# First pair's softmax ahead of the first weight conversion, and one more raw buffer, in a fused attention and two-stage MoE kernel

## Chip, cores and metric

The kernel runs on one core of a Trainium2 chip. The metric is the time of one execution on the device in microseconds. All times of the trace are microseconds from the start of the profiled span unless ns stands beside them. TensorE, VectorE, ScalarE and GpSimd are PE, DVE, ACT and POOL in the rows; SP issues the DMAs; PEld is the load of stationary operands.

## The reference, cut to what matters

```
scores = (q @ k.T) / 8; masked by blocks of 64 positions (block_i >= block_j)
attn   = softmax(scores) @ v                     # 4 batches, 8 heads, 576 x 64
x      = attn as [2304 tokens, 512]
x      = (sigmoid(x @ w_gate) * (x @ w_val)) @ w_out         # 512 -> 1536 -> 512
p      = domain_probs / (sum of domain_probs + 1e-9)
out    = sum over 4 experts e: p[:, e] * (relu(x @ w1[e]) @ w2[e])   # 512 -> 1024 -> 512
```

The inputs q, k and the MoE weights are float64 or float32 arrays; `w_gate`, `w_val` and `w_out` arrive as 64-bit words.

## The kernel before, in words

Three stages are interleaved on one core. **Attention** goes in 16 pairs of heads (4 batches of 4 pairs); a pair has query tiles t = 0 to 4 of 128 tokens (the last has 64). For each tile TensorE makes scores (line 350 for the first two batches), VectorE fills the masked corner (line 380) and takes the negative maximum (line 381, for t=4 line 411), ScalarE exponentiates with a running sum (lines 383, 416), TensorE transposes the probabilities (lines 459, 479), ScalarE copies them out of PSUM (line 446) and TensorE multiplies by v (line 532 through the helper at 119). Lines 491 to 510 prepare the inverse sums, line 541 writes the pair's output for batch 0. Steps of a pair are staggered: the transposes of a tile come three steps, the product with v four steps behind its scores, so steps of the next pair stand in between.

**The first MoE** works in four passes of 576 tokens (one batch each). Each pass has 12 blocks f of 128 hidden columns for gate and value. A block is one Winograd step of seven products; its weights come as four tiles a, b, c, d of high and low halves, made by `conv_items` (line 641): two raw blocks of 512 KB are loaded (line 647), decoded from 64-bit words by `from_f64` (lines 614 on ScalarE, 615 and 616 on VectorE), summed on GpSimd (line 662), split into high and low halves (`split_sb`, lines 124 to 133) and stored to DRAM (line 670) for later passes. Blocks 0 to 4 are converted during the attention of batch 0, the others during the first pass, which takes the blocks in the order `FIRST = (4, 0, 5, 1, 6, 2, 7, 3, 8, ...)`. Output weights are loaded raw and converted in `wo_get` (line 685). All raw tiles have the tag `raw` with three buffers in pool `conv`.

The operands of a pass are made by `x1_prep` (line 745) through `winograd_left`: four loads for each of two halves, sums on GpSimd (line 727), splits on ScalarE and VectorE (tiles `xc`). The first pass takes them from SBUF, the second pass loads them from DRAM into tiles `xr1` with four buffers (lines 752 to 757), the third and fourth have their own way (`x1_early`). **The second MoE** follows in three passes of 768 tokens.

What sets the order: the list `queue` holds the attention's steps with a place each (batch number plus the share of its cost so far); `attn_to(x)` runs them up to place x. At lines 1302 to 1305 the attention runs to place 0.12, and then the rest of batch 0 (to 1.05) is merged by cost with the 60 conversion steps of the first five blocks, 12 to a block. From there the attention is paced by the first MoE's progress (line 1359). Each engine executes its own instructions strictly in order; that order is drawn up when the kernel is built, by a planner that goes by the order in the text and a simulated timeline, so an instruction can be placed ahead of one that stands earlier in the text. A step wrapped in `pinned` (line 102) stays behind the instruction before it on VectorE, ScalarE and GpSimd. A tile's first writer waits until a buffer of its tag is free.

Of the kernel before, what the change touches and what calls it, by code (L numbers as in the profile page):

```python
# [8 lines left out]
F32 = mybir.dt.float32  # L9
F32R = mybir.dt.float32r  # L10
I32 = mybir.dt.int32
# [7 lines left out]
NC0 = 5  # L19
FIRST = (4, 0, 5, 1, 6, 2, 7, 3, 8, 9, 10, 11)  # L20
A00 = 0.12
A1 = [1.05, 2.3, 4, 4, 4]
PACE1 = 0.9
GB = 4
# [1 line left out]
LATE = (0, 1, 2)  # L26
LN = 1
ORD = "stvn"
RAW_BUFS = 3
PT2_BUFS = 1  # L30
LT, LP = 3, 4
PTB = 3
# [30 lines left out]
def attention_moe_moe_kernel(  # L63
# [18 lines left out]
    P = 128  # L82
    BLK = 64
    NKT = DM // P
    NF = DFF // P
# [50 lines left out]
    moe1 = tc.alloc_tile_pool(name="moe1", bufs=1)  # L136
    conv = tc.alloc_tile_pool(name="conv", bufs=1)
# [485 lines left out]
    TH1 = TP1 // 2  # L623
# [17 lines left out]
    def conv_items(f):  # L641

        d = {}

        def raw(gv):
            t = d["raw", gv] = conv.tile([P, NKT, P, 2], I32, tag="raw", name="raw", bufs=3)
            nc.sync.dma_start(
                out=t.rearrange("p c f t -> p c (f t)"),
                in_=(w_gate, w_val)[gv].bitcast(I32)[:, 2 * f * P:2 * (f + 1) * P].rearrange("(c p) f -> p c f", p=P))

        def f64(gv):
            d[gv] = from_f64(d["raw", gv].rearrange("p c f t -> p (c f) t"))

        def b(k, a):
            return d[a][:, k * QF:(k + 1) * QF]

        def sums(n):
            if n == 0:
                d["t"] = conv.tile([P, 4, QF], F32, tag="wt", name="wt")
            t = d["t"]  # L660
            x, y = [(b(0, 1), b(0, 0)), (b(1, 1), t[:, 0]), (b(1, 1), b(0, 1)), (b(1, 0), t[:, 1])][n]
            nc.gpsimd.tensor_tensor(out=t[:, n], in0=x, in1=y, op=ALU.subtract)

        def part(k):
            t = w1_tile(k)
            src = dict(a=lambda: d[0], b=lambda: d["t"][:, 0:2].rearrange("p n f -> p (n f)"),
                       c=lambda: d["t"][:, 2:4].rearrange("p n f -> p (n f)"), d=lambda: b(1, 1))[k]()
            split_sb(t[:, 0].rearrange("p n f -> p (n f)"), t[:, 1].rearrange("p n f -> p (n f)"), src,
                     "p" if k in "bc" else "a", "v" if k == "a" else "p")
            nc.sync.dma_start(out=w1_at(f, k), in_=t.bitcast(F32))  # L670
            if f >= NC0 - 1:
                wg[f, k] = t

        r = [lambda: raw(0), lambda: raw(1), lambda: f64(0), lambda: f64(1), lambda: sums(0), lambda: part("a"),
             lambda: sums(1), lambda: part("b"), lambda: sums(2), lambda: sums(3), lambda: part("c"), lambda: part("d")]
        return [(1.0, x) for x in r]
# [8 lines left out]
    def wo_get(p, f):  # L685
        t = wo[f] = moe1.tile([P, 2, DM], F32R, tag="wo", name="wo", bufs=4)
        if p:
            nc.sync.dma_start(out=t.bitcast(F32), in_=wo_d[f])
            return
        raw = conv.tile([P, NKT, P, 2], I32, tag="raw", name="raw", bufs=3).rearrange("p c f t -> p (c f) t")  # L690
        nc.sync.dma_start(out=raw.rearrange("p d t -> p (d t)"), in_=w_out.bitcast(I32)[f * P:(f + 1) * P, :])
        split_sb(t[:, 0], t[:, 1], from_f64(raw), "a", "p")
        nc.sync.dma_start(out=wo_d[f], in_=t.bitcast(F32))
# [18 lines left out]
    def winograd_left(pool, dst, load, n):  # L712
# [29 lines left out]
                    r.append((0.0, lambda kk=kk, m=m, key=key: part(kk, m, key)))  # L742
        return r

    def x1_prep(p):
        def load(kk, t, h):
            kt = h * KH + kk
            while (p, "b", kt) not in x_d:
                attn_next()
            if p == 0:  # L750
                return x0[kt][:, t]
            r = moe1.tile([P, TH1], F32, tag="xr1", name="xr1", bufs=4)
            if t == 0:
                nc.sync.dma_start(out=r[:, :QA], in_=x_d[p, "a", kt])
                nc.sync.dma_start(out=r[:, QA:], in_=x_d[p, "b", kt][:, :TH1 - QA])
            else:
                nc.sync.dma_start(out=r, in_=x_d[p, "b", kt][:, TH1 - QA:])
            return r

        return winograd_left(moe1, xc1, load, TH1)  # L760
# [145 lines left out]
    def run(lst):  # L906
        for _, fn in lst:
            fn()

    if True:  # L910
# [353 lines left out]
        for x in range(3):  # L1264
            t = (attn if x < 2 else pt2).tile([P, S], F32R, tag="kl" if x < 2 else "kl2", name=f"klz{x}", bufs=2 if x < 2 else 1)
# [3 lines left out]
        for x in range(2):  # L1269
            t = attn.tile([P, 5, 2, D], F32, tag="vh", name=f"vh{x}", bufs=2)  # L1270
            nc.vector.memset(t[64:128, 4], 0.0)
            vts.append(t)
        for x in range(PTB):
            t = (attn if x < 2 else pt2).tile([P, 1280], F32, name=f"pTb{x}")
# [23 lines left out]
        def attn_to(target):  # L1298
            while pos[0] < len(queue) and place[pos[0]] < target:
                attn_next()  # L1300

        attn_to(A00)
        a0 = [(queue[i][2], attn_next) for i in range(pos[0], len(queue)) if place[i] < A1[0]]
        cs = [conv_items(f) for f in range(NF)]
        _merge(a0, sum(cs[:NC0], []), 1.0)
        x_items = x1_prep(0)
        prev = []
        for p in range(NP1):
            at, total = 0.0, NF * 7 * 6 * C1 + NF * 2 * NKT * 3 * C1
            for f0 in range(0, NF, 2):  # L1310
                if (p, f0) == (NP1 - 1, 2):
                    x1b.release()
                    p2r = tc.alloc_tile_pool(name="p2r", bufs=1, side="right", reuse_waits="tile")
                    wp = [w_prep(0), w_prep(1)]
                    pre = x_prep(0) + [(0.0, lambda: (w_load(0), w_load(1), p_prep()))] + wp[0] + wp[1][:-2] + [(0.0, lambda: w2_load(0))]
                items = []
                for f in (f0, f0 + 1):
                    fa = order[p][f]
                    it = l1_1(p, fa)
                    side = []  # L1320
                    if (p, f) != (NP1 - 1, NF - 1):
                        nf = order[p][f + 1] if f + 1 < NF else order[p + 1][0]
                        if p == 0 and f + 1 < NF and nf >= NC0:
                            side += [x for _, x in cs[nf][HEAD:]]
                        else:
                            side.append(lambda nf=nf: w1_load(nf))
                    side.append(lambda fa=fa: wo_get(p, fa))
                    if p == 0 and f + 2 < NF and order[0][f + 2] >= NC0:
                        side += [x for _, x in cs[order[0][f + 2]][:HEAD]]
                    if p == NP1 - 1 and f >= 2:  # L1330
                        side += [pinned(x) for _, x in pre[len(pre) * (f - 2) // (NF - 3):len(pre) * (f - 1) // (NF - 3)]]
                    m = len(it)
                    steps = list(it)
                    for n in reversed(range(len(side))):
                        it.insert(1 + n * m // len(side), (0.0, side[n]))
                    if p in (1, 2) and f >= NF - 2:
                        if f == NF - 2:
                            if p == 1:
                                attn_to(99)
                                x1b = tc.alloc_tile_pool(name="x1b", bufs=1, side="right", reuse_waits="tile")  # L1340
                            first, part = x1_early(p + 1, x1b)
                            for n, fn in enumerate(first):
                                it.insert(1 + n, (0.0, fn))
                        else:
                            for n, x in enumerate(steps):
                                it.insert(it.index(x) + 1, (0.0, lambda n=n: part(ORD1[n])))
                    items += it
                if f0 == 0 and p < 2:
                    items = x_items + items
                if f0 == NF - 2 and p == 0:  # L1350
                    x_items = x1_prep(p + 1)
                    n = len(items)
                    for m in range(4):
                        items.insert(n * 2 // 3 + m, x_items[m])
                    x_items = x_items[4:]
                both = []
                _merge([(x[0], lambda x=x: both.append(x)) for x in items], [(x[0], lambda x=x: both.append(x)) for x in prev])
                for c, fn in both:
                    attn_to(A1[p] + (A1[p + 1] - A1[p]) * min(1.0, at / total / PACE1))
                    fn()  # L1360
                    at += c
                if (p, f0) == (0, NF - 2):
                    conv.release()
                prev = l2_1(p, f0)
        run(prev)
# [6 lines left out]
        for p in range(NPASS):  # L1372
            for q0 in range(0, NQ, 2):
# [22 lines left out]
                n = len(items)  # L1396
# [48 lines left out]
```

## Time and profile before

| what | before |
|---|---|
| median of 3 runs | 1411.94 us (1411.53 to 1413.97) |
| the profiled execution's own time | 1413.05 us |
| its span, first to last instruction | 1411.3 us |
| mean granted TensorE clock | 0.993 of full speed |
| busy: TensorE / its loads / VectorE / ScalarE / GpSimd | 1372.7 / 1267.3 / 986.3 / 777.6 / 481.5 us |
| DMA | 369.57 MB, 262 GB/s in the mean |

The profile is of one execution. Busy time of TensorE is modelled for pipelined matmuls and says little of how full it is where it waits often; the waits (in brackets in a timeline row: idle time before the instruction, and what ended it) say more.

### The profile page before, as it was taken

How to read it: one execution, taken by the hardware profiler on the slowest of the kernel's cores; microseconds unless marked ns; L12 is line 12 of the kernel's file. 1: busy time of each engine (PE TensorE's matmuls, PEld its weight loads, DVE VectorE, ACT ScalarE, POOL GpSimd, SP SyncE). 2: the span in 40 equal slices, each digit the busy share in tenths (PEclk: the TensorE clock that was granted, in tenths of full speed). 3: DMA queues.
4: the chain of work that ended last, by engine and by line, in shares of the span. 5: the costliest groups of instructions: out<-in, count | busy, mean ns of one | idle time of the engine just before them, and what ended most of it. 6: DMA issues, size and time to landing. Idle time of an engine off the chain costs nothing.

```text
span 1411.3 us, 26204 instructions
## 1 busy us (share of the span) xinstructions
PE 1372.7 (97%) x9212; PEld 1267.3 (90%) x9212; DVE 986.3 (70%) x2103; ACT 777.6 (55%) x1926; POOL 481.5 (34%) x502
## 2 busy tenths in 40 slices
PE   6899999999999999999999999999999999999998
PEld 3467787889988999999999999989999999999998
DVE  6877689976776445466777666757766787766766
ACT  5888788888876333343445444544444454443442
POOL 4753346301122200022576556533222342322322
PEclk8999999999999999999999999999999999999999
DMA  7999677886657877998799888886666777676754
GB/s 224 299 285 294 214 237 249 267 238 201 194 165 226 298 262 268 319 341 299 273 340 350 298 301 305 288 301 232 232 251 241 258 259 283 245 270 229 275 206 157
DMA packets 210803, 369.57 MB, mean 262 GB/s; under 512 B 74736, under 2 KB 137200, under 8 KB 204528
## 3 DMA queue, kind: packets, MB, share of 16 engines
q1 hardware_dynamic: 209584, 367.62, 77.2%
q8 instruction: 74, 1.21, 0.3%
q14 instruction: 57, 0.47, 0.1%
q10 hardware_dynamic: 1088, 0.26, 0.1%
HBM read 267.82 MB, written 100.01 MB: 261 GB/s over the span
## 4 chain that ended last, share of the span: by engine, by line
PE 86%; DVE 4%; DMA 4%; ACT 3%; issue 1%; SPq 1%; POOL 1%; DVEq 0%; ACTq 0%; POOLq 0%
PE c L119 38%; PE o L119 26%; PE lo L119 7%; PE s L119 4%; PE obank L119 3%; PE t L119 3%; PE tbank L459 2%; DMA raw<-in_moe_w_val_dram 1%; PE s L350 1%; PE tbank L230 1%; PE tbank L479 1%; DVE raw L616 1%; DMA w1g<-w1d 1%; DVE nm L381 0%; ACT pt L383 0%
## 5 line engine op out<-in xcount | busy, mean ns | idle before, releaser
L119 PE MATMUL c<-xc,w1g 128*128 128x384 f32 x1920 | 384.6, 338 | 1.5 <-DMA w1g<-w1d 1.2
L119 PEld LDWEIGHTS c<-xc,w1g 128*128 128x128 f32 x1920 | 330.5, 188 | 7.7 <-DVE hb L1073 1.4
L119 PE MATMUL o<-w2s,hb 128*128 128x256 f32 x1728 | 243.5, 282 | 1.1 <-DVE acc L1222 1.1
L119 PEld LDWEIGHTS o<-w2s,hb 128*128 128x128 f32 x1728 | 231.8, 189 | 2.0 <-DVE acc L1222 1.7
L1222 DVE SCALAR_TENSOR_TENSOR acc<-o,pr_t,acc 128x256 f32<-128x256 f32 x264 | 123.4, 479 | 57.9 <-PE o L119 55.8
L1082 POOL TENSOR_TENSOR hs<-hf 128x384 f32<-128x384 f32 x64 | 64.0, 1022 | 287.5 <-ACT hf L1090 256.4
L119 PE MATMUL lo<-g,wo 128*128 128x288 f32 x888 | 150.8, 301 | 5.0 <-DVE x L895 3.0
L119 PE MATMUL o<-w,hb 128*128 128x512 f32 x576 | 142.8, 391 | 0.0
L119 PEld LDWEIGHTS lo<-g,wo 128*128 128x128 f32 x888 | 126.4, 188 | 11.0 <-DVE x L895 5.1
L1090 ACT ACTIVATE hf<-c 128x384 f32<-128x384 f32 x128 | 65.7, 513 | 115.1 <-DVE c L1127 57.8
L119 PEld LDWEIGHTS o<-w,hb 128*128 128x128 f32 x576 | 107.2, 188 | 18.5 <-DVE acc L1166 0.2
L1127 DVE TENSOR_TENSOR c<-c,snap 128x384 f32<-128x384 f32 x144 | 77.8, 552 | 56.0 <-PE c L119 38.4
L1120 ACT ACTIVATE snap<-c 128x384 f32<-128x384 f32 x144 | 65.7, 484 | 87.1 <-PE c L119 86.8
L1071 ACT ACTIVATE hb<-hs 128x384 fp32r<-128x384 f32 x128 | 63.3, 518 | 64.4 <-POOL hs L1082 64.2
L1073 DVE TENSOR_TENSOR hb<-hs,hb 128x384 fp32r<-128x384 f32 x128 | 87.2, 696 | 5.5 <-ACT hb L1071 5.2
L895 DVE TENSOR_TENSOR x<-lo,x 128x288 f32<-128x288 f32 x124 | 55.7, 453 | 45.7 <-PE lo L119 44.9
L119 PE MATMUL c<-xc,wa 128*128 128x288 f32 x504 | 83.9, 300 | 1.8 <-ACT xc L131 1.6
L383 ACT ACTIVATE pt<-s,nm 128x128 f32<-128x128 f32 (+3 forms) x128 | 67.5, 529 | 17.9 <-DVE nm L381 10.7
L119 PEld LDWEIGHTS c<-xc,wa 128*128 128x128 f32 x504 | 71.8, 189 | 4.2 <-ACT xc L131 2.2
L119 PE MATMUL c<-xc,wc 128*128 128x288 f32 x432 | 70.8, 298 | 0.4 <-ACT snap L819 0.4
L819 ACT ACTIVATE snap<-c 128x288 f32<-128x288 f32 x108 | 44.4, 411 | 41.4 <-PE c L119 41.0
L459 PE MATMUL tbank<-ident,pt 128*128 128x128 f32 x320 | 53.6, 282 | 12.5 <-ACT pTa L446 7.7
(180 smaller groups left out, 2707.1 us busy)
## 6 DMA issues: line engine op xcount, KB each, us to landing
w1g<-w1d SPq DMA_DIRECT2D x96, 512.0 KB, 5.3
w2s<-w2d SPq DMA_DIRECT2D x48, 1024.0 KB, 6.2
w1d<-w1g SPq DMA_DIRECT2D x48, 512.0 KB, 4.9
wa<-w1d SPq DMA_DIRECT2D x40, 512.0 KB, 5.0
wb<-w1d SPq DMA_DIRECT2D x40, 512.0 KB, 5.1
wc<-w1d SPq DMA_DIRECT2D x40, 512.0 KB, 4.3
wo<-wod SPq DMA_DIRECT2D x36, 512.0 KB, 5.8
wr<-in_moe_w_dram SPq DMA_DIRECT2D x32, 512.0 KB, 5.4
```

The source lines that it names most:

```text
L119: ins = nc.tensor.matmul(out=out, lhsT=lhsT, rhs=rhs, start=start, stop=stop, skip_group_check=skip)
L383: ins = nc.scalar.activation(out=pt[:, x * nk:(x + 1) * nk], in_=sp[:, x - x0], func=AF.Exp, bias=nm[:, j0 + x:j0 + x + 1], scale=1.0, acc ...
L459: nc.tensor.transpose(out=tbank[:, x * P:(x + 1) * P], in_=pt[:, x * P:(x + 1) * P], identity=ident)
L819: nc.scalar.activation(out=t, in_=d["c1"][:, :TH1], func=AF.Copy)
L895: nc.vector.tensor_tensor(out=x2[t, dm], in0=ps, in1=x2[t, dm], op=ALU.add)
L1071: nc.scalar.activation(out=t[:, 0], in_=src, func=AF.Copy if low is None else AF.Relu)
L1073: nc.vector.tensor_tensor(out=t[:, 1], in0=src, in1=t[:, 0].bitcast(F32), op=ALU.subtract)
L1082: nc.gpsimd.tensor_tensor(out=o, in0=x, in1=y, op=op)
L1090: nc.scalar.activation(out=hf[q, blk], in_=c, func=AF.Relu)
L1120: nc.scalar.activation(out=t, in_=d["c1"][:, :TH], func=AF.Copy)
L1127: nc.vector.tensor_tensor(out=c, in0=d[tag][:, :TH], in1=d[n], op=ALU.add)
L1222: nc.vector.scalar_tensor_tensor(out=o, in0=ps, scalar=pr, in1=o, op0=ALU.mult, op1=ALU.add)
```

## The change

The attention runs to place 0.12, then the first block's two raw loads are issued, then the attention runs on to place 0.25 (`A01`), which takes in the last scores of pair 0, most of its transposes and the scores of pair 1's tiles 0 to 2. The remaining ten conversion steps of block 0 and all of blocks 1 to 4 are merged with the rest of batch 0's attention; block 0's two decoding steps are pinned behind what precedes them. The tag `raw` has four buffers. The second pass's operand loads lose their own tag: two of them share one raw tile (each takes 288 of its 1024 32-bit columns), and pool `conv` is released after the second pass's first pair of blocks instead of at the end of the first pass.

```diff
--- before.py
+++ after.py
@@ -19,6 +19,7 @@
 NC0 = 5
 FIRST = (4, 0, 5, 1, 6, 2, 7, 3, 8, 9, 10, 11)
 A00 = 0.12
+A01 = 0.25
 A1 = [1.05, 2.3, 4, 4, 4]
 PACE1 = 0.9
 GB = 4
@@ -26,7 +27,7 @@
 LATE = (0, 1, 2)
 LN = 1
 ORD = "stvn"
-RAW_BUFS = 3
+RAW_BUFS = 4
 PT2_BUFS = 1
 LT, LP = 3, 4
 PTB = 3
@@ -643,7 +644,7 @@
         d = {}
 
         def raw(gv):
-            t = d["raw", gv] = conv.tile([P, NKT, P, 2], I32, tag="raw", name="raw", bufs=3)
+            t = d["raw", gv] = conv.tile([P, NKT, P, 2], I32, tag="raw", name="raw", bufs=RAW_BUFS)
             nc.sync.dma_start(
                 out=t.rearrange("p c f t -> p c (f t)"),
                 in_=(w_gate, w_val)[gv].bitcast(I32)[:, 2 * f * P:2 * (f + 1) * P].rearrange("(c p) f -> p c f", p=P))
@@ -687,7 +688,7 @@
         if p:
             nc.sync.dma_start(out=t.bitcast(F32), in_=wo_d[f])
             return
-        raw = conv.tile([P, NKT, P, 2], I32, tag="raw", name="raw", bufs=3).rearrange("p c f t -> p (c f) t")
+        raw = conv.tile([P, NKT, P, 2], I32, tag="raw", name="raw", bufs=RAW_BUFS).rearrange("p c f t -> p (c f) t")
         nc.sync.dma_start(out=raw.rearrange("p d t -> p (d t)"), in_=w_out.bitcast(I32)[f * P:(f + 1) * P, :])
         split_sb(t[:, 0], t[:, 1], from_f64(raw), "a", "p")
         nc.sync.dma_start(out=wo_d[f], in_=t.bitcast(F32))
@@ -742,6 +743,8 @@
                     r.append((0.0, lambda kk=kk, m=m, key=key: part(kk, m, key)))
         return r
 
+    xw = {}
+
     def x1_prep(p):
         def load(kk, t, h):
             kt = h * KH + kk
@@ -749,7 +752,11 @@
                 attn_next()
             if p == 0:
                 return x0[kt][:, t]
-            r = moe1.tile([P, TH1], F32, tag="xr1", name="xr1", bufs=4)
+            if t == h:
+                t2 = conv.tile([P, NKT, P, 2], I32, tag="raw", name="xr1", bufs=RAW_BUFS)
+                xw[0] = t2.bitcast(F32).rearrange("p c f t -> p (c f t)")
+            o = 0 if t == h else TH1
+            r = xw[0][:, o:o + TH1]
             if t == 0:
                 nc.sync.dma_start(out=r[:, :QA], in_=x_d[p, "a", kt])
                 nc.sync.dma_start(out=r[:, QA:], in_=x_d[p, "b", kt][:, :TH1 - QA])
@@ -1300,8 +1307,11 @@
                 attn_next()
 
         attn_to(A00)
+        cs = [conv_items(f) for f in range(NF)]
+        run(cs[0][:2])
+        attn_to(A01)
+        cs[0] = [(c, pinned(fn) if n < 2 else fn) for n, (c, fn) in enumerate(cs[0][2:])]
         a0 = [(queue[i][2], attn_next) for i in range(pos[0], len(queue)) if place[i] < A1[0]]
-        cs = [conv_items(f) for f in range(NF)]
         _merge(a0, sum(cs[:NC0], []), 1.0)
         x_items = x1_prep(0)
         prev = []
@@ -1359,7 +1369,7 @@
                     attn_to(A1[p] + (A1[p + 1] - A1[p]) * min(1.0, at / total / PACE1))
                     fn()
                     at += c
-                if (p, f0) == (0, NF - 2):
+                if (p, f0) == (1, 0):
                     conv.release()
                 prev = l2_1(p, f0)
         run(prev)
```

## Rows read from the trace of the kernel before

**Rows 1.** TensorE's busy tenths in 40 slices of the span, on the page.

```profile
PE   6899999999999999999999999999999999999998
```

**Rows 2.** Busy us by stretch: PE, PEld, DVE, ACT, POOL (instructions), clock, DMA share, GB/s.

```profile
17.00:27.00 10.00, 3.11 (x16) 1.94 (x15) 9.30 (x19) 7.04 (x17) 7.03 (x8) 0.62 0.92 257
27.00:47.00 20.00, 16.65 (x97) 9.41 (x95) 18.40 (x45) 15.76 (x49) 15.64 (x18) 0.85 0.91 301
47.00:67.00 20.00, 17.00 (x113) 9.66 (x114) 16.77 (x51) 16.65 (x57) 13.42 (x15) 1.00 0.94 286
67.00:87.00 20.00, 17.81 (x116) 10.81 (x116) 16.59 (x42) 16.88 (x54) 14.76 (x17) 1.00 1.03 344
107.00:200.00 93.00, 91.69 (x645) 73.52 (x645) 70.11 (x180) 75.92 (x214) 34.52 (x35) 1.00 0.79 253
200.00:280.00 80.00, 76.07 (x549) 66.87 (x548) 74.27 (x178) 69.04 (x189) 36.66 (x35) 1.00 0.78 256
```

**Rows 3.** Timeline, opening: start, length, engine, line, what [idle before, releaser].

```profile
12.44 3.89 PE L350 MATMUL s<-tkn,tqn 64*64 64x288 f32 x12
...
16.93 0.43 DVE L615 TENSOR_SCALAR raw<-raw 128x512 int32<-128x512 int32 x1 [3.66 <-DMA raw<-in_moe_w_gate_dram]
...
17.27 0.45 DVE L411 TENSOR_REDUCE nm<-s 128x1 f32<-128x288 f32 x1
...
23.30 0.38 SPq L647 DMA_DIRECT2D raw<-in_moe_w_val_dram  x1
...
24.03 0.90 PE L459 MATMUL tbank<-ident,pt 128*128 128x128 f32 x3 [6.89 <-ACT pTa L446]
...
27.58 0.67 ACT L614 ACTIVATE raw<-raw 128x512 f32<-128x512 f32 x1 [1.10 <-DMA raw<-in_moe_w_val_dram]
...
34.75 0.56 DVE L381 TENSOR_REDUCE nm<-s 128x1 f32<-128x384 f32 x1
```

**Rows 4.** Timeline: block 4's last weights on POOL, and first pass products on TensorE.

```profile
73.34 1.28 POOL L133 TENSOR_TENSOR wc<-wt,wc 128x512 fp32r<-128x512 f32 x1
...
90.85 0.64 PE L119 MATMUL c<-xc,wa 128*128 128x288 f32 x3
...
97.26 1.02 PE L119 MATMUL c<-xc,wc 128*128 128x288 f32 x6 [0.41 <-ACT snap L819]
```

**Rows 5.** Groups of ScalarE, 13 to 46 us: busy, mean ns; idle before.

```profile
L383 ACT ACTIVATE pt<-s,nm 128x384 f32<-128x384 f32 (+3 forms) x12 | 6.7, 561 | 1.0 <-DVE nm L381 1.0
...
L446 ACT ACTIVATE pTb<-tbank 128x384 f32<-128x384 f32 (+3 forms) x9 | 3.5, 425 | 0.0
...
L383 ACT ACTIVATION_READ_ACCUMULATOR pt<-s,nm 128x1 f32 x12 | 2.5, 205 | 0.0
...
L416 ACT ACTIVATE pt<-s,nm 128x288 f32<-128x288 f32 x4 | 2.0, 496 | 2.4 <-DVE nm L413 2.4
```

**Rows 6.** Groups of VectorE, 0 to 87 us, same columns.

```profile
L381 DVE TENSOR_REDUCE nm<-s 128x1 f32<-128x128 f32 (+3 forms) x36 | 16.5, 470 | 0.5
...
L616 DVE SCALAR_TENSOR_TENSOR raw<-raw 128x512 int32<-128x512 int32 x13 | 10.8, 840 | 0.3
...
L615 DVE TENSOR_SCALAR raw<-raw 128x512 int32<-128x512 int32 x13 | 7.2, 551 | 3.9 <-DMA raw<-in_moe_w_gate_dram 3.8
...
L133 DVE TENSOR_TENSOR wa<-raw,wa 128x512 fp32r<-128x512 f32 x5 | 4.8, 960 | 0.0
```

**Rows 7.** The raw tiles, whole span: ns min/median/max, first and last start.

```profile
L615 DVE TENSOR_SCALAR raw<-raw x36: 412/424/1491, 16.9 to 252.7; 128x512 int32<-128x512 int32 x36
...
L616 DVE SCALAR_TENSOR_TENSOR raw<-raw x36: 660/692/1659, 17.6 to 253.3; 128x512 int32<-128x512 int32 x36
...
L647 SPq DMA_DIRECT2D raw<-in_moe_w_val_dram x12: 368/384/972, 12.4 to 232.0; - x12
...
DMA to landing us min/median/max: 3.6/5.3/8.2
```

**Rows 8.** Tile xr, 90 to 300 us: first split of the second pass's operands.

```profile
L131 ACT ACTIVATE xc<-xr x6: 443/454/496, 263.0 to 276.9; 128x288 fp32r<-128x288 f32 x6
```

## The prediction

> **What bounds the kernel now.** I read the page first, for where TensorE is not full. Its row of 40 slices stands at 9 from the third slice to the last but one and is lower only in the first two [rows 1]: what can be won lies in the opening 70 us and in the first pass's start behind them. Next, the windows [rows 2]. From 27 to 87 us TensorE is nominally 83 to 89% busy, but VectorE is the fuller one at first (18.40 of 20 us from 27 to 47) and close to it later (16.77 and 16.59); from 107 us on TensorE is full. So the opening is a matter of VectorE and ScalarE, both with strict order, and after it the time is TensorE's: what the first pass starts earlier, the end comes earlier, unless a later stretch takes it back.
>
> Then the timeline of the opening [rows 3]. VectorE waits 3.66 us, from 13.27 to 16.93, for the first raw gate block: line 615 stands ahead of line 411 in its order, although TensorE's 12 score products of t=4 and t=3 began at 12.44. ScalarE waits for the same block. TensorE gets its next probabilities' transposes only at 24.03, after 6.89 us of nothing. In 17 to 27 us VectorE is 9.30 of 10 busy, but with the conversion. The granted clock there is 0.62: part of that stretch ran at 1.2 instead of 2.4 GHz.
>
> Last, who needs what at the first pass's start [rows 4]. The first block (f=4) has its last pair of weights when the POOL instruction of 73.34 us ends, 74.62. The second product, which needs the fourth pair's output, resumes at 90.85, and the product that needs those last weights runs at 97.26. So the conversion is some 20 us early and the attention is what the pass waits for. The change moves time from the first to the second.
>
> **The change part by part.**
>
> *Order.* The softmax of pair 0 (t=4, t=3) and pair 1's first three query tiles go ahead of the first conversion, whose two decoding steps are pinned behind them. Attention first. The t=4 scores allow the two line-411 maxima from about 14.6, so that ScalarE's exponentials begin near 15.9. Between them and the pin ScalarE has eight line-383 exponentials (8 x 0.561), two of line 416 (2 x 0.496), ten accumulator reads of 0.205 of which half lies inside the exponential, nine copies of line 446 (9 x 0.425), and five small ones of lines 506, 238 and 263 (1.8) [rows 5]: 4.5 + 1.0 + 1.0 + 3.8 + 1.8 = 12.1 us. The first decoding step so starts near 28.0 us, 11.1 later than 16.93. The maxima of pair 1's t=2 tile, which end at 35.31 now [rows 3], would end near 26.3: the attention is 9.0 us ahead there. That is the upper bound of the gain; the lower one is below nothing, if the late conversion is what the pass then waits for.
>
> Between these I go by VectorE's time up to the fourth pair's end (87 us now), in three terms.
> (a) Work that goes behind that point. Five blocks run from 16.93 to 74.62 us, 11.5 us each. A block costs VectorE 2 x (0.551 + 0.840) + 0.960 = 3.74 us, and by 87 us 13 decodings are done where five blocks need 10 [rows 6]. 11.1 us later is 0.97 of a block: 3.6 us come after the fourth pair instead of before. Bounds: 0 and 4.2 (the three surplus decodings, 3 x 1.39).
> (b) A new gap. From 13.27 to 28.0 us VectorE has eight maxima of 0.470, two of 0.45 and, by my estimate, some 2.9 us of fills and small ones: 7.5 of 14.7 us, so 7.2 idle. Now it idles 3.66 + 0.70 + about 0.1 = 4.4 there. Minus 2.8; bounds -2.8 and 0, since the second block's decoding is not pinned and can fill gaps.
> (c) Gaps filled later. With conversion always waiting, as from 27 to 47 us now, VectorE should stay at 92%. From 47 to 87 us it is busy 33.36 of 40; at 92% the same work takes 36.3, that is 3.7 less; I take 3.4, as the fourth pair's last chain can't be filled. Bounds 0 and 6.6 (no idle time).
> Sum: 3.6 - 2.8 + 3.4 = 4.2 us.
> What (a) puts off falls in 107 to 200 us, where VectorE idles 93 - 70.1 = 23 us: nothing, as long as it is used up before 200; in 200 to 280 us, with VectorE at 74.27 of 80 and TensorE idle 3.9 [rows 2], it would cost up to its length.
>
> *Queues.* Both raw loads of the first block are issued by 12.4 us already [rows 7]; in the new text they pass no other load, so SP loses nothing. They land within 8.2 us, by 20.6: the pinned steps at 28 wait for no load, and nothing queues behind them in vain. The first block's four stores go behind pair 2's loads on SP; they are read back only for the first pass's second block. POOL begins its conversion work near 30 instead of near 20; it has 50.9 us of work from 17 to 87 us, so at most some 10 in each of five blocks, which fits into 11.5.
>
> *Fourth raw buffer.* The second block's second load is issued at 23.30 and kept ScalarE waiting 1.10 us at 27.58 [rows 3]. With a buffer free it can follow the first at once, and is there long before it is decoded: this is part of (c), not added.
>
> *Operand blocks of the second pass in the raw buffers.* Now they have four of their own and the first halves are loaded long ahead; the first split runs at 263.0 us [rows 8]. In the new order they take a buffer when the raw blocks before them have theirs; the last value block is issued at 232.0, output blocks behind it. Issued by some 250 and landed 8.2 later they are there before 263: I take 0, with bounds of -1 (a part of the 3.9 us that TensorE idles from 200 to 280) and +2 (a buffer free at 257 only). The release of the pool comes two steps later, and nothing takes its memory there: nothing.
>
> A place for a rule: line 615 takes 0.424 us in the median but 1.491 at worst, line 616 0.692 and 1.659 [rows 7]; up to 87 us their means are 0.551 and 0.840. That excess, 13 x 0.127 + 13 x 0.148 = 3.6 us, falls where POOL works beside them. The Trainium skill (SBUF — State Buffer, Who interferes with whom) says that VectorE and GpSimd share a port pair that one of them holds for a whole instruction while the other is blocked; it speaks against packing the same POOL work into less time. The worst durations agree with it in kind; no row here shows which instruction held the other up. I keep the excess as it is in the sum; as a rival, below, it doubles.
>
> 4.2 us off the profiled execution's own 1413.05 (span 1411.3) is 1408.85; that execution lay 1.1 above the median, so for the median of runs I take 1411.94 - 4.2 = **1407.7 us**. What a measurement can tell from no change is 0.2%, 2.8 us.
>
> **The rivals.**
> 1. *The lead is kept whole*: the pairs go on at their own pace, 9.0 us early, and conversion is late but early enough. For: 20 us of spare time. Against: VectorE can't do the same work in 9 us less, only 8 us of idle time lie from 27 to 87. 1411.94 - 9.0 = 1402.9.
> 2. *VectorE's work is conserved*, and the change does not do what it says: with four buffers the second block's unpinned decodings slip ahead, or the later gaps don't fill. (c) is gone: 3.6 - 2.8 = 0.8, so 1411.1. For: the maxima wait for TensorE's scores and transposes too, not for work.
> 3. *The port*: the excess doubles, 4.2 - 3.6 = 0.6, so 1411.3. For: POOL is busy 50.9 of the 70 us from 17 to 87 and would have 55 for them. Against: the maxima of line 381, read from PSUM, are the larger part of what moves.
> 4. *Slower: the first pass waits for weights.* The five blocks start at 28.0. At 11.5 us each they end at 85.7 and are needed at 97.26 - 4.2 = 93.1. Attention now goes first in the text, so they may get less: from 13.0 us a block the gain shrinks, at 13.9 it is gone, and at 15 they end at 103.0, 5.7 us behind 97.26: 1417.6. For: blocks later in the first pass take some 20 us each (twelve value loads from 12.4 to 232.0 us). Against: the gaps of (c) are theirs.
>
> **How the numbers follow.** Forecast 0.45, lead kept 0.13, conserved 0.17, port 0.07, weights late 0.18. Faster: 0.45 + 0.13 = 0.58; same: 0.17 + 0.07 = 0.24; slower: 0.18. The forecast's own range is 1405 to 1409; toward both sides I go to 1402.5 (the lead kept) and 1415.0 (conserved with the worst of (b) and the handover, and the milder part of rival 4).
>
> **What would show it.** Right: lines 411 and 413 before line 615 in VectorE's order, without the 3.66 us wait; TensorE's gap of 6.89 us gone or under 3; decoding from about 28; the fourth pair's end and the first pass's resumption 4 us earlier, and the same 4 us at every later pass. Wrong: the resumption as early as hoped but waits for weights or for VectorE between 100 and 280 us; a wait for operand blocks near 265; or maxima of pair 1 that are early while those of pair 4 are not.

## The result and the profile after

The changed kernel takes 1421.56 us (median of 6 runs, 1417.10 to 1422.68) against 1411.74 (6 runs, 1409.65 to 1413.97) beside it on the same chip: ratio 1.0062, 95% interval 1.0050 to 1.0074. It is slower by 9 to 10 us where the forecast was 4 us faster, and the time lies outside the range. The profiled execution took 1422.59 us, its span 1420.8, the mean granted clock 0.994 (0.993 before).

TensorE's slices on the page: the second and the third fall by one against [rows 1], the rest stays.

```profile
PE   6789999999999999999999999999999999999998
```

The windows of after, for the stretches of [rows 2] and for 87 to 107 us (before: TensorE 19.06, VectorE 15.19, GpSimd 8.75 there):

```profile
17.00:27.00 10.00, 4.07 (x18) 2.64 (x19) 4.57 (x11) 4.58 (x11) 0.00 (x0) 0.69 0.70 177
27.00:47.00 20.00, 17.75 (x118) 9.97 (x117) 15.24 (x47) 17.49 (x58) 8.72 (x10) 0.98 0.41 107
47.00:67.00 20.00, 14.72 (x83) 8.88 (x82) 17.04 (x33) 13.33 (x35) 17.13 (x20) 0.83 1.04 338
67.00:87.00 20.00, 15.40 (x101) 9.20 (x100) 17.61 (x47) 16.76 (x56) 14.28 (x17) 1.00 0.87 286
87.00:107.00 20.00, 16.54 (x106) 10.06 (x104) 15.99 (x37) 14.78 (x42) 10.29 (x11) 1.00 1.03 337
107.00:200.00 93.00, 91.45 (x648) 73.71 (x649) 77.81 (x183) 77.42 (x219) 42.36 (x40) 1.00 0.79 264
200.00:280.00 80.00, 73.14 (x522) 64.33 (x521) 72.19 (x167) 65.13 (x178) 39.96 (x38) 1.00 0.79 250
```

From 17 to 27 us VectorE is half idle (4.57 where before had 9.30), up to 47 us TensorE does 2 us more than before (21.82 against 19.76), and from 47 to 107 us it does less: 14.72, 15.40 and 16.54 where before had 17.00, 17.81 and 19.06. The opening's work was pushed back and came due together.

The opening of after, timelines of VectorE, ScalarE, TensorE and GpSimd (answers to [rows 3]; line numbers near the top of the kernel are one higher than before):

```profile
14.05 1.03 DVE L412 TENSOR_REDUCE nm<-s 128x1 f32<-128x288 f32 x2 [0.44 <-PE s L351]
...
21.66 0.43 DVE L616 TENSOR_SCALAR raw<-raw 128x512 int32<-128x512 int32 x1 [3.35 <-DMA raw<-in_moe_w_gate_dram]
...
31.80 0.55 DVE L382 TENSOR_REDUCE nm<-s 128x1 f32<-128x384 f32 x1
32.26 0.42 DVE L616 TENSOR_SCALAR raw<-raw 128x512 int32<-128x512 int32 x1
```

```profile
21.66 0.68 ACT L615 ACTIVATE raw<-raw 128x512 f32<-128x512 f32 x1 [3.32 <-DMA raw<-in_moe_w_gate_dram]
22.23 0.59 ACT L447 ACTIVATE pTa<-tbank 128x512 f32<-128x512 f32 x1
...
34.16 0.68 ACT L615 ACTIVATE raw<-raw 128x512 f32<-128x512 f32 x1
```

```profile
22.88 0.90 PE L460 MATMUL tbank<-ident,pt 128*128 128x128 f32 x3 [6.44 <-ACT pTa L447]
```

```profile
38.28 2.10 POOL L663 TENSOR_TENSOR wt<-raw 128x256 f32<-128x256 f32 x2 [35.80 <-DVE raw L617]
```

The softmax of the first pair is early, as meant: the maxima of line 412 run at 14.05. But the decoding at 21.66, with a step on VectorE and one on ScalarE, is not the first block's. It is that of the *second* block's gate half, whose load went out at 17.38 into the third buffer, and it stands ahead of the copy of line 447 on ScalarE. (The fourth buffer let only the value half follow at once, at 17.93; 23.30 in before.) Both engines wait over 3.3 us for that load, the copy behind it is late, and TensorE has its gap of 6.44 us after all (6.89 before). The first, pinned block is decoded only at 32.26, and GpSimd begins its conversion work at 38.28 instead of 19.88.

The handover to the first pass (answers to [rows 4]; GpSimd, then VectorE's last output of the fourth pair, 89.11 before, then TensorE):

```profile
92.00 1.27 POOL L134 TENSOR_TENSOR wc<-wt,wc 128x512 fp32r<-128x512 f32 x1
```

```profile
94.80 0.49 DVE L542 TENSOR_TENSOR x<-obank,xr 128x320 f32<-128x320 f32 x1
```

```profile
95.82 0.40 PE L120 MATMUL c<-xc,wa 128*128 128x288 f32 x1 [1.00 <-ACT xc L132]
...
105.50 1.04 PE L120 MATMUL c<-xc,wc 128*128 128x288 f32 x6
...
109.05 0.95 PE L120 MATMUL c<-xc,wd 128*128 128x288 f32 x6
```

The last weights are there at 93.27 and used at 105.50: nobody waits for them. The attention itself is 5.7 us late, and from its last output to the first product with wd it takes 14.25 us instead of 12.30 (101.41 less 89.11). So 7.6 us are lost by 109 us. The first store of the first pass's output is 7.6 us late too (291.48 against 283.88), that of the fourth pass 6.6 (681.64 against 675.09); another 2.6 us go in the second MoE (last section). The span is 9.5 us longer.

### The profile page after: what moved, and what is told of

The parts are those of the page before. It is cut to its first block, busy times and chain, and to the rows that moved or that the text cites. A ratio compares the mean times of both kernels' runs of the same rounds, so it can differ in the third digit from the quotient of the medians.

```text
span 1420.8 us, 26186 instructions
## 1 busy us (share of the span) xinstructions
PE 1372.9 (97%) x9212; PEld 1268.0 (89%) x9212; DVE 996.4 (70%) x2103; ACT 779.7 (55%) x1926; POOL 484.2 (34%) x502
## 4 chain that ended last, share of the span: by engine, by line
PE 88%; DVE 5%; DMA 3%; ACT 1%; issue 1%; POOL 1%; SPq 1%; ACTq 0%; DVEq 0%; POOLq 0%
PE c L120 38%; PE o L120 26%; PE lo L120 7%; PE s L120 4%; PE obank L120 3%; PE t L120 3%; PE tbank L460 2%; PE s L351 2%; PE tbank L231 1%; DMA raw<-in_moe_w_gate_dram 1%; DVE raw L616 1%; PE tbank L480 1%; DVE xc L134 0%; DVE nm L382 0%; DVE x L902 0%
## 5 line engine op out<-in xcount | busy, mean ns | idle before, releaser
L728 POOL TENSOR_TENSOR xs<-xr 128x384 f32<-128x384 f32 (+1 forms) x14 | 15.1, 1078 | 152.4 <-DMA xr<-x2d 114.5
```

## The experiments

In the tables "last output" is the start of VectorE's last output of the fourth pair, "first wd" the first product with wd, "pass 1" the first store of the first pass's output, "pass 4" that of the fourth; all from the timelines of the profiled executions. The times are medians and the four columns one execution each, which in e3, e7, c2 and c3 lay 3 to 6 us off the median (1418.98, 1426.83, 1415.01 and 1412.52 us): the columns tell where time goes rather than how much of the median. The change: 94.80, 109.05, 291.48, 681.64; before: 89.11, 101.41, 283.88, 675.09.

**First, the halves.** Theories: A, the second block's decodings slip ahead; B, the lead of 0.25 is too long; C, the shared buffers cost in the first pass. A step n of 2 or 3 of a block is a decoding. The edits, against after except for the order alone, which is the change's hunk at line 1302 put into before:

```diff
# e1
+        cs[1] = [(c, pinned(fn) if n in (2, 3) else fn) for n, (c, fn) in enumerate(cs[1])]
# e5: e1, and
-A01 = 0.25
+A01 = 0.155
# e2: without the hunk at line 1302
# e3: before, and
+        run(cs[0][:2])
+        attn_to(A01)
+        cs[0] = [(c, pinned(fn) if n < 2 else fn) for n, (c, fn) in enumerate(cs[0][2:])]
```

Second block pinned as well:

> The changed kernel, with the second block's two decoding steps pinned in their place of the text as well, so that they cannot stand ahead of the first block's. Theory A (the loss comes from the second block's decoding that slips ahead, stalls VectorE and ScalarE for 3.35 us at 18.3 us and leaves the first block waiting): the stall goes, the first decoding starts near 26 us instead of 34.2, and the time is at or below 1414. Theory B (the loss comes from the long lead itself: POOL has no conversion work until 38 us, and five blocks have then to be squeezed beside the attention of the pairs 1 to 3): the stall goes, but POOL still starts near 30 us or later and no block is decoded earlier in sum; 1418 to 1424. Theory C (the shared raw buffers cost the time, later in the first pass): no change from 1421.6.

Buffers only:

> The kernel before with the buffer part alone: four raw buffers, the second pass's operands in them, the later release; order of the opening as before. Theories A and B: the opening is as before or slightly better (the wait of 1.10 us for the second raw block goes), 1409 to 1413. Theory C: most of the loss is here, 1417 or more, with TensorE idle between 200 and 280 us.

Order only:

> The kernel before with the order part alone: lead to place 0.25, first block's decoding pinned, three raw buffers, operands of the second pass in their own four. The second block's gate half still slips ahead (it has the third buffer), its value half can't. Theory A: half of the slip and the same stall, 1416 to 1421. Theory B: as the changed kernel or worse, 1419 to 1425, since with three buffers even less conversion is at hand. Theory C: 1408 to 1413.

Short lead, two blocks pinned:

> The changed kernel with a short lead: the attention runs ahead only to place 0.155 (pair 0's last scores and no more of pair 1), both first blocks' decoding pinned. Theory A: no stall, so at or below 1412. Theory B: conversion starts near 20 us, softmax of pair 0 is 3 to 4 us earlier than before, so the first pass starts earlier than before: 1406 to 1411. Theory C: still 1418 or more.

| | us, ratio to before (interval) | last output | first wd | pass 1 | pass 4 |
|---|---|---|---|---|---|
| e1 | 1419.07, 1.0045 (1.0029 to 1.0062) | 89.61 | 107.05 | 294.29 | 682.99 |
| e2 | 1422.25, 1.0064 (1.0049 to 1.0079) | 96.63 | 111.30 | 296.83 | 681.29 |
| e3 | 1423.10, 1.0068 (1.0050 to 1.0086) | 86.78 | 105.33 | 292.92 | 680.12 |
| e5 | 1421.18, 1.0059 (1.0044 to 1.0074) | 89.66 | 106.47 | 287.33 | 680.56 |

Either half alone costs 9 us (0.64 and 0.68%), and together they cost no more. None of A, B and C carries it alone: pinning the second block takes the slipped decoding away (the last output comes 5.2 us earlier than in the change), but the ratio only falls from 1.0062 to 1.0045; and e5 stayed at 1421.2, where A and B gave 1412 at most. The two halves lose in different places. The buffers alone make the attention late (96.63). The order alone brings it 2.3 us *early* and loses the time behind it, 18.55 us from the last output to the first wd. It does so with the change's own stall in the opening, and with three buffers (VectorE's timeline of e3):

```profile
21.90 0.43 DVE L616 TENSOR_SCALAR raw<-raw 128x512 int32<-128x512 int32 x1 [3.19 <-DMA raw<-in_moe_w_gate_dram]
```

So this stall needs no fourth buffer, and by itself it does not make the attention late. Behind the last output TensorE waits 3.1 us in all in e3 (from 86 to 106 us; 0.8 from 89 to 102 in before), of which 1.2 are for the last block's weights; the rest of the longer stretch is not settled. The waits for the weights:

```profile
96.55 0.79 PE L120 MATMUL c<-xc,wb 128*128 128x288 f32 x4 [0.43 <-POOL wb L130]
99.94 1.33 PE L120 MATMUL c<-xc,wb 128*128 128x288 f32 x8 [0.76 <-POOL wb L134]
```

**Second, is it the tail, the decodings' places, or any other order?**

```diff
# e6: e3 with, and e7: before with
-NC0 = 5
-FIRST = (4, 0, 5, 1, 6, 2, 7, 3, 8, 9, 10, 11)
+NC0 = 4
+FIRST = (3, 0, 4, 1, 5, 2, 6, 7, 8, 9, 10, 11)
# e8: e2, and
+        cs[:NC0] = [[(c, pinned(fn) if n in (2, 3) else fn) for n, (c, fn) in enumerate(x)] for x in cs[:NC0]]
# e9: before with
-A00 = 0.12
+A00 = 0.20
```

Order alone, four blocks ahead of the first pass:

> The order part alone with three raw buffers, as in the run of the order alone, but only four blocks are converted ahead of the first pass (it then begins with block 3; block 4 is converted in the first pass). Theory T, the tail: in the order alone the fourth pair's last output was even 2.3 us early (86.78 against 89.11), but the last block's conversion then ran beside the splits of the operands, and from there to the first product with wd it took 18.6 us where before took 12.3. With one block less, the step from the last output to that product takes at most 14 us and the time is 1408 to 1415, if the first pass has room for the block (VectorE idles 23 us from 107 to 200). Theory R, the order drawn up before is simply a well tuned one and every other order costs 6 to 10 us: 1418 to 1424. Theory W, only the last block's weights come too late and the rest of the loss is elsewhere: the step shortens but the time stays at 1418 or more.

Before, four blocks:

> The kernel before with four blocks converted ahead of the first pass instead of five, nothing else: the control for the run above. T: before has its conversion done 15 us ahead of the fourth pair's end, so the tail costs it nothing; the attention can gain at most the block's VectorE time (3.74 us), the first pass has a block more: 1409 to 1416. R: 1418 to 1424, as it is another order too.

Buffers alone, all five blocks pinned:

> Buffers alone (four raw buffers, operand blocks in them, old place of the first conversion), with the decoding steps of all five blocks held in the order of the text. Theory H, the fourth buffer lets the order put decodings ahead of the attention, which made the fourth pair's last output 7.5 us late (96.63 against 89.11) in the run of the buffers alone: pinned, that output comes by 91 and the time is at most 1417. R: 1419 to 1424. Theory C, the shared buffers themselves cost: the attention is in time by 91 but the first or second pass loses, 1418 or more.

Before, attention to 0.20, nothing pinned:

> The kernel before with the attention run to place 0.20 instead of 0.12 ahead of the conversion; nothing is pinned, three raw buffers. Both maxima of line 411 then stand ahead of the first decoding on VectorE, and the decodings still slip between the softmax steps: the smallest form of the change's order. T: a short lead without a late conversion costs no tail: 1407 to 1414, with the last output by 89. R: 1418 to 1424.

| | us, ratio (interval) | last output | first wd | pass 1 | pass 4 |
|---|---|---|---|---|---|
| e6 | 1422.66, 1.0070 (1.0054 to 1.0085) | 89.38 | 106.94 | 293.49 | 684.80 |
| e7 | 1421.36, 1.0062 (1.0043 to 1.0081) | 87.95 | 100.42 | 299.88 | 686.59 |
| e8 | 1415.39, 1.0016 (1.0005 to 1.0027) | 83.60 | 99.92 | 288.57 | 674.80 |
| e9 | 1426.22, 1.0084 (1.0068 to 1.0100) | 93.54 | 105.69 | 292.04 | 687.59 |

Theory T fell in e6, e7 and e9, in the form I gave it: with one block less the stretch behind the last output is still 17.56 us, because the *next* block's unpinned decodings at once take the room (VectorE's line 616 at 89.79 and 93.04, between the operands' splits). Theory H held: with the same buffers and all decodings kept in the order of the text, the last output comes 13.0 us earlier than without (83.60 against 96.63) and of the 8.8 us lost against its own before (1413.5) 3.0 are left (against 1412.42). Theory R, that every other order costs 6 to 10 us, is refuted by this run, but e7 and e9 show that it is often so: e9 drew nothing but another order and lost 14 us; e7, in a profiled execution 5.5 us above its median, was 1.0 us ahead of before at the first wd and 16.0 behind at the first pass's store, in a pass with one block more to convert.

**Third, the same pins on the change, on a short lead and on before; and the shared tiles alone.**

```diff
# b1: after, and behind the cs[0] line
+        cs[1:NC0] = [[(c, pinned(fn) if n in (2, 3) else fn) for n, (c, fn) in enumerate(x)] for x in cs[1:NC0]]
# b2: b1 with
-A01 = 0.25
+A01 = 0.155
# b3: before with the line of e8
# b5: e2 with
-RAW_BUFS = 4
+RAW_BUFS = 3
```

The change, all five blocks pinned:

> The change with the decoding steps of all five early blocks held in the order of the text, not only the first block's two. Theory H, the loss comes from decodings that the order puts ahead of softmax steps (the pinning gave the buffers alone 7 us back): the fourth pair's last output comes by 88 instead of 94.80 and the time is 1410 to 1417. Theory L, a lead as long as this makes the conversion end too late whatever its order: the output may come early, but the first product with wd stays at 105 or later and the time at 1418 to 1423. Theory R, every other order costs 6 to 10 us: 1418 to 1424.

Short lead, all five pinned:

> The same with the attention run to 0.155 instead of 0.25 ahead of the first decoding: the first pair's softmax alone goes ahead. H and L both: 1408 to 1415, with the last output by 86 and the first product with wd by 101; better than the run above by 2 or more if L holds. R: 1418 to 1424.

Before, all five pinned:

> The kernel before (three raw buffers, old place of the first conversion, operand tiles of their own) with the decoding steps of all five blocks held in the order of the text. H: what the order of decodings is worth without the fourth buffer: 1409 to 1415, about as the buffers alone pinned (1415.4), better by the 2 to 3 us that the shared buffers may cost in the first pass. R: 1418 or more.

Three buffers, shared with the operand blocks:

> The kernel before with three raw buffers in which the second pass's operand blocks take turns as in the change, and the later release; no fourth buffer, no other order of the conversion. Its instructions stand as before up to about 100 us. Theory C, the sharing itself costs in the first pass: the same as before up to 101 us, then 3 to 6 us lost by 290, 1415 to 1420. Theory H: the sharing is worth -1 to +3, 1411 to 1415, and the 9 us of the buffers alone come from the fourth buffer by way of the order. R: 1418 or more though the opening is unchanged.

| | us, ratio (interval) | last output | first wd | pass 1 | pass 4 |
|---|---|---|---|---|---|
| b1 | 1424.56, 1.0087 (1.0072 to 1.0102) | 88.08 | 110.63 | 298.45 | 687.04 |
| b2 | 1412.26, 1.0001 (0.9992 to 1.0011) | 81.33 | 97.65 | 286.40 | 672.76 |
| b3 | 1420.31, 1.0052 (1.0040 to 1.0065) | 84.87 | 98.44 | 291.44 | 683.08 |
| b5 | 1411.65, 0.9997 (0.9987 to 1.0006) | 89.82 | 102.14 | 285.78 | 675.52 |

The shared tiles cost nothing: theory C is out, and what the buffers alone lose comes from the fourth buffer. With the short lead the five pins bring the time back to that of before (b2), with the long one they do not (b1, 1.6 us above what theory L gave): the lead's length counts. b3 missed its theory: with three buffers at the old place the same pins bring the last output 4.2 us early, and the time is 8 us longer, lost in the first pass. In b1 GpSimd gets its first decoded block at 33.95 us (19.88 in before). Most of its waits from 27 to 112 us is that one wait of 31.5 us, which began at 2.5,

```profile
POOL wt L663 <- DVE raw L617: 36.0, 2, 31.5
```

and the last block's weights are then made between the sums that the first pass's own operands need (line 728):

```profile
92.79 1.48 POOL L134 TENSOR_TENSOR wb<-wt,wb 128x512 fp32r<-128x512 f32 x1
94.66 0.79 POOL L728 TENSOR_TENSOR xs<-xs,x 128x288 f32<-128x288 f32 x1 [0.40 <-DVE xc L134]
95.42 0.62 POOL L130 TENSOR_SCALAR wc<-wt 128x512 fp32r<-128x512 f32 x1
96.12 1.27 POOL L134 TENSOR_TENSOR wc<-wt,wc 128x512 fp32r<-128x512 f32 x1
```

That these weights come late is not enough to explain the longer stretch of b1: they end 9.3 us behind the last output, and in b2 9.5 us behind it (90.85). What differs is that TensorE waits 6.5 us in that stretch (3.0 in b2), and that its clock fell there, 0.68 from 88 to 98 us (1.00 from 81 to 98 in b2). Through which step a long lead costs is not shown.

In b2 the opening looks as the change meant it. ScalarE's copy has no decoding ahead of it, TensorE's gap is 2.45 us, and the window keeps the full clock; the first row is TensorE's timeline, the second its window of 17 to 27 us:

```profile
18.66 0.55 PE L460 MATMUL tbank<-ident,pt 128*128 128x128 f32 x3 [2.45 <-ACT pTa L447]
```

```profile
17.00:27.00 10.00, 7.47 (x54) 4.45 (x54) 7.21 (x25) 8.82 (x29) 2.31 (x3) 1.00 0.73 190
```

**Fourth, the square of lead and pins, and whether more pins keep the gain.**

```diff
# e4: after with
-A01 = 0.25
+A01 = 0.155
# c2: b1 with A01 = 0.20
# c3: b2 with RAW_BUFS = 3 and the operand tiles xr1 of before
# c1: b2 with cs[1:] instead of cs[1:NC0]
```

The change with the short lead:

> The change with the lead cut from place 0.25 to 0.155, its pinning as it is (the first block's two decodings). Theory H+L, both causes, each enough by itself: the other blocks' decodings still go ahead of softmax steps, 1418 to 1424. Theory L alone, only the lead's length counts: 1410 to 1415, as with all pinned.

Lead 0.20, all five pinned:

> All five blocks' decodings held, the lead at place 0.20. L: the conversion's start moves back with the lead and its end with it, so the time lies between 1412.3 (0.155) and 1424.6 (0.25): 1415 to 1421, the first product with wd at 101 to 107. If the lead's length does not count: 1410 to 1414, and the run at 0.25 lost for another reason.

Short lead, all five pinned, three buffers:

> The short lead with all five blocks held, with three raw buffers and the operand tiles of their own as before. If the fourth buffer pays once decodings are held (as 1415.4 against 1420.3 at the old place suggests): 1416 to 1422. If it does nothing there: 1410 to 1415.

Short lead, all twelve pinned:

> The short lead with four buffers and the decodings of all twelve blocks held in the order of the text, the first pass's too. H: the 3.8 us lead at the first product with wd is kept in part through the first pass: 1407 to 1411. If the first pass loses it for another reason (TensorE is full there): 1411 to 1414. If the first pass needs its decodings early: 1415 or more.

| | us, ratio (interval) | last output | first wd | pass 1 | pass 4 |
|---|---|---|---|---|---|
| e4 | 1432.07, 1.0130 (1.0110 to 1.0151) | 98.42 | 116.58 | 305.74 | 692.95 |
| c2 | 1418.44, 1.0033 (1.0017 to 1.0049) | 85.47 | 104.70 | 287.40 | 677.74 |
| c3 | 1416.07, 1.0022 (1.0007 to 1.0036) | 83.54 | 97.09 | 285.72 | 675.09 |
| c1 | 1413.55, 1.0009 (0.9992 to 1.0026) | 83.52 | 99.90 | 289.15 | 676.95 |

c2 and c3 came out in the first of their theories, c1 in its second; e4 is slower than either of its two. Both the pins and the lead show by themselves. At the short lead, with four buffers, the pins go 1432.1 (first block), 1421.2 (two), 1412.3 (five). With five blocks pinned, the lead goes 1412.3 (0.155), 1418.4 (0.20), 1424.6 (0.25), and the stretch from last output to first wd goes 16.3, 19.2, 22.6 us. In e4 the second block's decoding stalls ScalarE even longer than in the change, and TensorE with it:

```profile
22.33 0.69 ACT L615 ACTIVATE raw<-raw 128x512 f32<-128x512 f32 x1 [4.43 <-DMA raw<-in_moe_w_gate_dram]
22.92 0.58 ACT L447 ACTIVATE pTa<-tbank 128x512 f32<-128x512 f32 x1
```

```profile
23.56 0.90 PE L460 MATMUL tbank<-ident,pt 128*128 128x128 f32 x3 [7.57 <-ACT pTa L447]
```

No version beat the kernel before. The best with another order, b2, is 3.8 us ahead at the first wd and 2.3 at the fourth pass, and level at the end: the 2.3 go where the second MoE's first pass hands over to its second (last section). Pinning the first pass's decodings as well (c1) did not keep the lead. Why the first pass takes 6 us longer in b2 (189 us from first wd to its first store, 182 in before; the next three win most of it back) is not settled; before with pins (b3) loses 10.5 there.

## Why the prediction was wrong

**What bounds the kernel: right.** The first pass resumes 1.0 us behind the attention's last output (1.7 before), weights ready, in after as in before. Of the 9.5 us of span, 5.7 are the attention's own lateness.

**The step that failed first: "the second block's decoding is not pinned and can fill gaps".** It stood as the reason why (b) could not be worse than -2.8 us. A decoding put into a gap *ahead* of its data is a wait for everything behind it on a strictly ordered engine. I did not ask where the next block's decodings can be placed, though that was the premise of my own second rival. VectorE idles 12.0 us from 13 to 47 us (busy 2.17 + 4.57 + 15.24 of 34) where before had 6.0: (b) is -6.0. The first block is decoded from 32.26 instead of 28.0, and the t=2 maxima end at 32.35 instead of 26.3: a lead of 3.0 us, not 9.0. TensorE's gap stayed.

**The larger part: the lead was not kept.** The starts of each pair's last output (128x320, line 541, from VectorE's timelines):

| | first pair | second | third | fourth |
|---|---|---|---|---|
| before | 43.34 | 58.07 | 74.75 | 89.11 |
| the change | 39.71 | 58.87 | 77.73 | 94.80 |
| e3, order alone | 39.42 | 55.03 | 71.72 | 86.78 |
| e1, second block pinned too | 33.88 | 52.83 | 70.65 | 89.61 |

With its first pair the change is still 3.6 us ahead; it loses 9.3 us from there to the fourth. e3 has the same stall and loses 1.6. In e1 the opening comes out as forecast, the t=2 maxima ending at 26.28 and the first decoding at 26.20:

```profile
25.73 0.55 DVE L382 TENSOR_REDUCE nm<-s 128x1 f32<-128x384 f32 x1
26.20 0.42 DVE L616 TENSOR_SCALAR raw<-raw 128x512 int32<-128x512 int32 x1
```

Its first pair is 9.5 us ahead, and of these nothing is left at the fourth. So the opening was priced rightly for an order that holds; what (a) and (c) said of the 50 us behind it was wrong.

**(a), work put behind the fourth pair: 3.6 predicted, 1.4 measured.** The window up to the fourth pair's last output, 0 to 89.2 us in before and 0 to 94.9 in after (VectorE's busy time is the third), and VectorE's groups from 0 to 94.9 us in after (answers to [rows 6]; before decodes nothing between 87 us and its last output):

```profile
0.00:89.20 89.20, 68.55 (x397) 38.94 (x397) 67.95 (x183) 63.67 (x197) 52.63 (x65) 0.92 0.90 273
```

```profile
0.00:94.90 94.90, 70.38 (x407) 40.59 (x407) 68.93 (x179) 65.29 (x197) 49.65 (x61) 0.93 0.77 228
```

```profile
L617 DVE SCALAR_TENSOR_TENSOR raw<-raw 128x512 int32<-128x512 int32 x12 | 10.2, 848 | 0.6 <-ACT raw L615 0.3
L616 DVE TENSOR_SCALAR raw<-raw 128x512 int32<-128x512 int32 x12 | 10.1, 838 | 3.8 <-DMA raw<-in_moe_w_gate_dram 3.7
...
L381 DVE MEMSET s<- 64x64 f32 x36 | 3.9, 112 | 10.4 <-PE s L351 10.2
```

By 87 us 21 decoding steps are done where before had 26, about as predicted, but the next three run at 87.71 to 91.4, ahead of the fourth pair's last output. Twelve block halves (gate or value) are decoded ahead of it, 13 in before: 1.4 us of work went behind (0.551 + 0.840), not 3.6. The last row shows the other side: VectorE's fills waited 10.2 us for TensorE's scores (7.7 in before).

**(c), gaps filled later: +3.4 predicted, -1.1 measured.** From 47 to 87 us VectorE is busy 34.65 us of 40, not 36.8 (92%), that is 1.3 more than before. But up to the last output it is busy 1.0 us more than before (68.93 against 67.95) with 1.4 us of work less, so 2.4 of its time is stretch, not work. The stretch is that of line 616, which took 838 ns in the mean instead of 551, 3.4 us over 12 steps; other groups became shorter. The Trainium skill (SBUF — State Buffer, Who interferes with whom) says that one of VectorE and GpSimd can hold a shared port pair for a whole instruction while the other is blocked. The trace agrees, and its rows show which instruction held the step up (last section). Against the medians of the whole span (432 and 692 ns) the excess of the decoding steps is 12 x (838 - 432) + 12 x (848 - 692) = 6.7 us, with 3.6 before: nearly the doubling that the third rival named, of which 0.7 is won back elsewhere.

By VectorE the sum becomes 1.4 - 6.0 + 1.3 - 2.4 = -5.7 us, which is what the last output is late. This is a balance of one engine: it tells which terms were wrong, not that VectorE alone caused it. Behind it come 2.0 us in the handover, which had no term at all, since I took the way from last output to first products as fixed. The runs show it at 12.2 to 22.6 us.

**Rivals.** The second named the slip of the opening but priced it as conserved work (1411.1): waits are not conserved. The fourth, weights late, did not happen in the change (93.27 against 105.50); that a longer lead costs more holds in the series of leads. Its direction came out (1417.6 against 1421.6), its cause did not.

**Operand blocks in the raw buffers, 0 (-1 to +2): right.** b5 gives 0.9997. Their first split moved with the pass [rows 8]:

```profile
L132 ACT ACTIVATE xc<-xr x6: 432/434/442, 271.4 to 280.9; 128x288 fp32r<-128x288 f32 x6
```

8.4 us later, where the pass itself is 7.6 late. **Fourth buffer, part of (c): wrong.** Alone it costs 9 us by way of the order, and only with the decodings pinned does it pay (1415.4 against 1420.3 at the old place, 1412.3 against 1416.1 at the short lead).

**The range** ended at 1415.0 because the bounds of (a) to (c) were made of work and idle time of one engine. A stall ahead of the critical copy was in none of them, nor was time lost in the handover or in the second MoE (2.6 us).

## What to carry to other kernels

When an order is drawn up by a planner, another buffer is also a permission: look up what may now be placed earlier, and on which strictly ordered engine it will wait for its data ahead of the chain that matters. Moving critical work ahead is worth little if the rest is left free to fill in: here pinning one or two blocks was not enough, and pinning all five brought the short lead level with before (though in the kernel before itself the same pins cost 8 us). A lead won in the opening has to be followed stage by stage to the handover: e1 had 9.5 us of it and ended slower. And a delayed background stage has a far end: price what it meets there, with the lead as the variable, and take the smallest lead that removes the wait.

## What the runs showed of the hardware

The rows show the decoding step of line 616 held up by GpSimd. In after four of these steps, at 47.56, 53.02, 64.48 and 67.11, take 1.30 to 1.50 us (0.43 in the median), and each ends 0.28 us behind the GpSimd subtraction of line 134 that had begun before it. The last two, on GpSimd and on VectorE:

```profile
64.43 1.27 POOL L134 TENSOR_TENSOR wb<-wt,wb 128x512 fp32r<-128x512 f32 x1
...
66.55 1.58 POOL L134 TENSOR_TENSOR wc<-wt,wc 128x512 fp32r<-128x512 f32 x1
```

```profile
64.48 1.50 DVE L616 TENSOR_SCALAR raw<-raw 128x512 int32<-128x512 int32 x1
...
67.11 1.30 DVE L616 TENSOR_SCALAR raw<-raw 128x512 int32<-128x512 int32 x1
```

From 47 to 87 us the step's mean is 418 ns in before, 416 in b5 and 484 in e3, all with three buffers; it is 1055 in after, 896 in e1 and 783 in e2, with four. With all five blocks pinned it is 540 to 696 ns, with three buffers as with four.

At the handover inside the second MoE, TensorE's wait was 1.19 us in before, with the clock at 1.00 from 940 to 960 us. In after it was 2.29 us, and the window from 950 to 960 us shows 0.83, so part of it ran at 1.2 GHz:

```profile
951.70 3.34 PE L120 MATMUL c<-xc,w1g 128*128 128x384 f32 x12 [2.29 <-DVE c L1134]
```

```profile
950.00:960.00 10.00, 8.30 (x41) 8.33 (x42) 4.69 (x11) 4.02 (x9) 2.59 (x3) 0.83 0.84 298
```

The same 12 products took 3.34 us instead of 2.35. From the end of the second MoE's first pass to the first output store of its second it took 235.7 us (944.00 to 1179.69) against 233.1 (937.26 to 1170.34): 2.6 us, of which 1.1 is the longer wait. b2 waits 2.5 us at the same place, also shows 0.83 (940 to 950 us), and also takes 2.6 us longer there (935.00 to 1170.70). But its wait of 2.45 us in the opening left the clock at 1.00, so the length of a wait alone does not decide it.

Single executions of one kernel roughly followed the granted clock: with twelve blocks pinned, 1409.27 us at a mean clock of 0.999 and 1420.88 at 0.991.
